# Moving columns of the up-projection in alternating runs, and padded w_in tiles, in a block-sparse attention + MLP kernel

## The chip, the cores and the metric

The kernel runs on one NeuronCore of a Trainium2 chip. The metric is device time in microseconds (us) for one execution. Engine names are those of the profile: PE is TensorE's matmul, PEld its weight load, DVE is VectorE, ACT is ScalarE, POOL is GpSimd, SP is SyncE, whose queue issues most of the DMAs.

## The reference

Block-sparse attention over 4 sequences of 768 tokens, 8 heads of 64, followed by a two-layer MLP on the 3072 tokens:

```python
scores = scale * np.matmul(q, k.transpose(0, 1, 3, 2))
...
attn_out = np.matmul(attn, v).astype(np.float32)
x = np.ascontiguousarray(attn_out.transpose(0, 2, 1, 3)).reshape(B * S, H * D)   # 3072 x 512
h = x @ w_in                                   # 512 -> 2048
g = h * (1.0 / (1.0 + np.exp(-1.702 * h)))
return (g @ w_out).astype(np.float32)          # 2048 -> 512
```

The mask keeps the first and last block row and column, the neighbours of the diagonal, and three sampled blocks per block row.

## The kernel before

The 3072 tokens are taken in NC = 6 chunks of CT = 512. The attention of a chunk is cut into items (scores, transposes, values, turn) that are laid between the steps of the MLP of the chunk before it, by a table (`plan`) in program order; the first chunk's attention comes ahead of the MLP in a handwritten order (`first`). TensorE executes its instructions in that written order.

The MLP runs over m = 0 to 95: m = 16 c + f, where c is the chunk and f one of NF = 16 slices of the 2048 hidden features. For each m, `up` makes h (128 features x 512 tokens) in one PSUM bank, `gate` applies the gelu (tanh on ACT, a product on DVE), `gate_hi` and `gate_lo` split the result in two, and one step later `down` multiplies it by w_out and sums over f in four other banks. The split into a high part (fp32r) and a low part is how single-pass matmuls reach the accuracy of fp32: a product is hi\*hi + hi\*lo + lo\*hi.

So one `up` is 4 values of k (128 rows of the 512 features each) times 3 matmuls (L565, L566, L567), 12 matmuls, each with a stationary 128 x 128 block of a w_in tile and 512 moving columns of x; the six chunks make 96 x 12 = 1152 of them. A w_in tile `win{f}` holds, in each partition, 1024 fp32 values: four 128-wide blocks of the high part, then four of the low part. The moving rows xhi and xlo (tile x1 in odd chunks) are 512 fp32 values, 2 KB, for each k. Both operands are read, and h is written, from front to back.

The tiles live in one SBUF pool that puts them one behind the other in the order in which they are made. A tile "pad" of 56 values near the front makes every large tile before the change start at a multiple of 2048 bytes; the w_in tiles stand there in the order win15 to win10, then win0 to win9, 4096 bytes each. The tiles win15 to win10 also lend their space, early on, to gathered value blocks (`spare` in `__init__`), before w_in arrives there.

Of the kernel before, what the change touches and what calls it, by code (L numbers as in the profile page):

```python
# [9 lines left out]
F32 = mybir.dt.float32  # L10
F32R = mybir.dt.float32r
I32 = mybir.dt.int32
# [6 lines left out]
P = 128  # L19
# [5 lines left out]
DM = H * D  # L25
DF = 2048
NCT = DM // P
NF = DF // P
# [13 lines left out]
AHEAD = 5  # L42
NFULL = 8
FIRST = CU // 2
ORDER = """X1 G0 G1 G2 G3 S0 S1 L0 E0 L1 X2 T0 E1 S2 S3 L2 C0 T1 C1 Y1 V0 N0 L3 X3 V1 E2 T2 R0 N1 E3 H0 S4 R1 S5 C2 T3 L4 H1
V2 N2 E4 C3 L5 Y2 T4 C4 R2 H2 E5 V3 N3 S6 L6 R3 G4 S7 H3 L7 E6 T5 V4 C5 Y3 V5 N4 E7 W W R4 T6 C6 N5 W R5 H4 H5 T7 C7 W
V6 N6 W V7 W R6 N7 H6 R7 H7 W W"""
# [2 lines left out]
class Kernel:  # L50
# [4 lines left out]
    def __init__(self, ctx, tc, q, qd, kb, kT, v, vd, sb, w_in, w_out, out):  # L55
        self.tc, self.nc = tc, tc.nc
        self.q, self.qd, self.kb, self.kT, self.v, self.vd, self.sb = q, qd, kb, kT, v, vd, sb
        self.w64, self.out = (w_in.bitcast(I32), w_out.bitcast(I32)), out
        pool = lambda name, bufs, **k: ctx.enter_context(tc.tile_pool(name=name, bufs=bufs, **k))
        self.const = pool("const", 1)  # L60
        self.work = pool("work", 2)
        self.small = pool("small", 6)
        psum = pool("psum", 1, space=PSUM)
        dram = pool("dram", 1, space=DRAM)
        self.ws = [dram.tile([P, DM], F32, name=f"ws{f}") for f in range(NF)]
        self.bank = [psum.tile([P, 512], F32, name=f"bank{i}") for i in range(8)]
        c = self.const


        self.sbr = c.tile([1, NB, NR, 2], I32, name="sbr")  # L70
        self.zero = c.tile([P, 1], F32, name="zero")
        self.seen = c.tile([P, 2 * NPAIR], F32, name="seen")
        self.ident = c.tile([P, P], F32, name="ident")
        self.vidx = c.tile([P, 2, NB], I32, name="vidx")
        self.bias = c.tile([P, NU, 8], F32, name="bias")
        c.tile([P, 56], F32, name="pad")

        self.kg = [c.tile([P, 12, 2, NPAIR * BLK], F32, name=f"kg{i}") for i in range(RING)]
        self.qt = [c.tile([P, 2, NPAIR * UT], F32, name=f"qt{i}") for i in range(RING)]
        self.vown = [c.tile([P, 2, 2 * DM], F32, name=f"vown{i}") for i in range(RING)]  # L80
        self.vmid = [c.tile([P, 2 * DM], F32, name=f"vmid{i}") for i in range(RING)]
        self.win = [None] * NF
        self.x = [tuple(c.tile([P, NCT, CT], F32R, name=f"x{part}0") for part in ("hi", "lo"))]


        more = c.tile([P, 2 * NCT * CT], F32, name="x1")
        nk, nq = 24 * NPAIR * BLK, 2 * NPAIR * UT
        for flat in (more[:, 0:nk], c.tile([P, 2 * WRING * DM], F32, name="wout")):
            self.kg.append(flat.rearrange("p (n b c) -> p n b c", n=12, b=2))
        self.qt += [more[:, nk + nq * i:nk + nq * (i + 1)].rearrange("p (b c) -> p b c", b=2) for i in range(2)]  # L90
        spare = [c.tile([P, 2 * DM], F32, name=f"win{NF - 1 - i}") for i in range(6)]
        self.vblocks = [[t[:, j] for j in range(2)] for t in self.vown] + [spare[0:2], spare[2:4]]
        self.vmid += spare[4:6]
        self.kmidof, self.vmidof = [None] * FIRST, [None] * FIRST
        self.units, self.kent, self.vent, self.items = [], [], [], []

        def entry(of, **more):
            of.append({"n": len(of), "scores": 0, "values": 0, **more})
            return of[-1]

        def item(k, v, **more):
            k["scores"] += 1
            v["values"] += 1
            self.items.append({"n": len(self.items), "unit": self.units[-1], "k": k, "v": v, **more})

        for b0 in range(0, B, 2):
            for u in range(NU):
                k, v = (entry(of, b=b0, u=u) for of in (self.kent, self.vent))
                for b in (b0, b0 + 1):
                    entry(self.units, b=b, u=u)  # L110
                    item(k, v, first=True, end=True)
            for b in (b0, b0 + 1):
                entry(self.units, b=b, u=None)
                k = entry(self.kent, b=b, u=None)
                for i in range(2):
                    v = entry(self.vent, b=b, u=None, i=i)
                    for half in range(2):
                        item(k, v, i=i, half=half, first=i + half == 0, end=i + half == 2)
        for of in (self.kent, self.vent):
            for e in of:  # L120
                e["at"] = e["n"] if e["n"] < FIRST else e["n"] % RING
        self.knext = self.vnext = FIRST
        self.most = {"scores": FIRST + 1, "values": FIRST + 1}
        self.early, self.turned = True, False
# [73 lines left out]
    def load_k(self, e):  # L198
# [18 lines left out]
        self.sampled(e, 0, nc.sync)  # L217
        if e["n"] >= FIRST or e["n"] == 0:
            self.sampled(e, 1, nc.sync if e["n"] else nc.scalar)
# [237 lines left out]
    def weights(self):  # L457

        nc = self.nc
# [7 lines left out]
        tiles = {}  # L467

        def fetch(k):
            if k < len(todo):  # L470
                f, i = todo[k]
                if i == 0:
                    raw = self.const.tile([P, 2 * DM], I32, name=f"win{f}")
                else:
                    raw = self.work.tile([P, 2 * DM], I32, name="raw", bufs=3)
                nc.gpsimd.dma_start(out=raw, in_=self.w64[i][f])
                tiles[k] = {"raw": raw.rearrange("p (a b) -> p a b", b=2)}
# [25 lines left out]
        for k, (f, i) in enumerate(todo):  # L503
            fetch(k + AHEAD)
            raw, a = tiles[k]["raw"], tiles[k]["a"]
            low, high = raw[:, :, 0], raw[:, :, 1]
            nc.vector.tensor_scalar(out=a, in0=a, scalar1=3, scalar2=None, op0=ALU.logical_shift_left)
            yield
            if k > 0 and "to" in tiles[k - 1]:
                rest(k - 1)  # L510
                yield
            nc.vector.scalar_tensor_tensor(out=a, in0=high, scalar=-0x80000000, in1=a, op0=ALU.bitwise_and,
                                           op1=ALU.bitwise_or)
            if k + 1 < len(todo):
                while todo[k + 1][1] == 1 and (not self.turned or todo[k + 1][0] - (4 if todo[k + 1][0] < NFULL else WRING) > self.downs - 1):
                    yield
                first(k + 1)
            yield
            w = a if (i, f >= NFULL) != (1, True) else raw.rearrange("p a b -> p (a b)")[:, 0:DM]
            nc.vector.scalar_tensor_tensor(out=w, in0=low, scalar=29, in1=a, op0=ALU.logical_shift_right,  # L520
                                           op1=ALU.bitwise_or)
            w = tiles[k]["w"] = w.bitcast(F32)
            if i == 0:
                self.win[f] = tiles[k]["to"] = self.const.tile([P, 2 * DM], F32R, name=f"win{f}")
            else:
                nc.sync.dma_start(out=self.ws[f], in_=w)
                if f < NFULL:
                    self.whole[f] = w
                    self.ready.add((f, i))
                else:  # L530
                    tiles[k]["to"] = self.wout[f % WRING]
            if "to" in tiles[k]:
                nc.scalar.copy(out=tiles[k]["to"][:, 0:DM], in_=w)
            yield
# [15 lines left out]
    def split(self, m):  # L550
        if m in self.wst:
            w, t = self.wst.pop(m), self.wout[m % WRING]
            self.nc.scalar.copy(out=t[:, 0:DM], in_=w)  # L553
            self.nc.vector.tensor_tensor(out=t[:, DM:2 * DM], in0=w, in1=t[:, 0:DM].bitcast(F32), op=ALU.subtract)  # L554

    def up(self, m, ks):
        nc = self.nc
        c, f = divmod(m, NF)
        if c == 0:
            self.need(f, 0)  # L560
        hi, lo = self.x[c % 2]
        wih, wil = (self.win[f][:, DM * k:DM * (k + 1)].rearrange("p (k m) -> p k m", k=NCT) for k in range(2))
        h = self.bank[2 if m == 1 else (7, 0)[m % 2] if c == NC - 1 else 7]
        for k in ks:
            nc.tensor.matmul(h, wih[:, k], hi[:, k], start=(k == 0), stop=False)  # L565
            nc.tensor.matmul(h, wih[:, k], lo[:, k], start=False, stop=False)  # L566
            nc.tensor.matmul(h, wil[:, k], hi[:, k], start=False, stop=(k == NCT - 1))  # L567
        self.h = h

    def gate(self, m, between):  # L570
# [323 lines left out]
```

## Time and profile before

| | |
|---|---|
| median of 2 runs | 761.75 us (761.07 to 762.42) |
| profiled execution | 762.78 us, of which the span from first to last instruction is 761.1 us |
| PE busy | 732.3 us, 96% of the span |
| DVE, ACT busy | 406.7 us (53%), 375.4 us (49%) |
| granted TensorE clock, mean | 0.992 |

In the profile a duration of a matmul runs from its start to the end of its drain, so that the durations of neighbours overlap. What a stream of matmuls costs is read from start to start, not from the durations. "Idle before" is time that the engine stood still ahead of an instruction, and the arrow names what ended it.

### The profile page before, as it was taken

The numbers are of one execution on the slowest core, as the hardware profiler recorded it, in microseconds if no ns is written. First come the engines' busy times: TensorE is split into PE (matmuls) and PEld (weight loads), VectorE is DVE, ScalarE is ACT, GpSimd is POOL, SyncE is SP. The second block draws the span as 40 slices with busy tenths as digits, with TensorE's granted clock in tenths as the row PEclk, the third lists the DMA queues.
The fourth block names the chain that finished last, engine by engine and source line by source line (L and its number), as shares of the span: only waits on it lengthen the run. The fifth ranks groups of instructions, "written<-read, shape, count | busy, mean of one in ns | idle before, by whom it ended". The sixth has DMA issues, their size and how long they took to land.

```text
span 761.1 us, 18922 instructions
## 1 busy us (share of the span) xinstructions
PE 732.3 (96%) x7424; PEld 564.8 (74%) x7424; DVE 406.7 (53%) x1069; ACT 375.4 (49%) x938; POOL 68.6 (9%) x111
## 2 busy tenths in 40 slices
PE   3779999999999999999999999999999999999997
PEld 2565666777787777778878878878777777888885
DVE  4578988895554434554454554454554444443333
ACT  3565667775554443544444545445545444333232
POOL 4332122020000000000000000000000000000000
PEclk9899999999999999999999999999999999999999
DMA  8998996775742547555435455435564331141111
GB/s 241 301 373 320 342 314 213 244 227 178 255 160 70 170 138 206 161 170 171 126 120 171 135 166 170 129 114 176 159 218 155 90 105 29 41 105 49 50 48 56
DMA packets 64251, 126.88 MB, mean 167 GB/s; under 512 B 7617, under 2 KB 30402, under 8 KB 63650
## 3 DMA queue, kind: packets, MB, share of 16 engines
q1 hardware_dynamic: 51922, 83.72, 36.3%
q0 software_dynamic: 11376, 41.03, 15.9%
q8 instruction: 58, 0.95, 0.5%
q10 hardware_dynamic: 864, 0.93, 0.4%
q14 instruction: 31, 0.25, 0.1%
HBM read 115.16 MB, written 10.49 MB: 165 GB/s over the span
## 4 chain that ended last, share of the span: by engine, by line
PE 92%; DMA 2%; SPq 2%; DVE 1%; issue 1%; ACT 1%; DVEq 0%
PE bank L565 13%; PE bank L566 11%; PE bank L567 11%; PE bank L624 10%; PE bank L625 10%; PE bank L620 10%; PE bank L354 6%; PE bank L378 6%; PE bank L303 5%; PE bank L610 4%; PE bank L398 2%; PE bank L315 2%; DMA x<-in_kb_dram 1%; PE bank L443 1%; SPq L225 1%
## 5 line engine op out<-in xcount | busy, mean ns | idle before, releaser
L580 DVE SCALAR_TENSOR_TENSOR g<-g,bank 128x512 f32<-128x512 f32 x83 | 57.0, 687 | 181.7 <-ACT g L573 181.7
L338 ACT ACTIVATE ex<-bank,nm 128x256 f32<-128x256 f32 (+1 forms) x176 | 84.6, 490 | 117.1 <-DVE nm L326 117.1
L624 PE MATMUL bank<-wout,ghi 128*128 128x512 f32 x352 | 139.8, 397 | 0.0
L625 PE MATMUL bank<-wout,ghi 128*128 128x512 f32 x352 | 137.2, 390 | 0.0
L573 ACT ACTIVATE g<-bank 128x512 f32<-128x512 f32 x96 | 57.3, 597 | 148.2 <-PE bank L567 148.2
L554 DVE TENSOR_TENSOR wout<-wst,wout 128x512 fp32r<-128x512 f32 x80 | 55.4, 692 | 79.9 <-ACT wout L553 78.8
L620 PE MATMUL bank<-wout,glo 128*128 128x512 f32 x352 | 97.1, 389 | 0.0
L326 DVE CUSTOM_DVE_ANT_1 bank<-bank,bias 128x256 f32<-128x256 f32 x176 | 73.7, 440 | 17.1 <-PE bank L303 10.5
L565 PE MATMUL bank<-xhi,win 128*128 128x512 f32 x192 | 80.3, 418 | 0.5 <-ACT xhi L450 0.5
L587 ACT CAST ghi<-g 128x512 fp32r<-128x512 f32 x88 | 54.7, 621 | 50.4 <-DVE g L580 50.4
L565 PE MATMUL bank<-x,win 128*128 128x512 f32 x192 | 78.3, 408 | 0.2 <-DVE g L580 0.2
L620 PEld LDWEIGHTS bank<-wout,glo 128*128 128x128 f32 x352 | 66.1, 188 | 13.9
L624 PEld LDWEIGHTS bank<-wout,ghi 128*128 128x128 f32 x352 | 66.1, 188 | 13.5
L625 PEld LDWEIGHTS bank<-wout,ghi 128*128 128x128 f32 x352 | 66.2, 188 | 13.0
L566 PE MATMUL bank<-xlo,win 128*128 128x512 f32 x192 | 75.4, 393 | 0.0
L567 PE MATMUL bank<-xhi,win 128*128 128x512 f32 x192 | 75.3, 392 | 0.0
L567 PE MATMUL bank<-x,win 128*128 128x512 f32 x192 | 75.1, 391 | 0.0
L566 PE MATMUL bank<-x,win 128*128 128x512 f32 x192 | 75.1, 391 | 0.0
L255 POOL DMA_INDIRECT vown<-in_v_dram,vidx x40 | 38.6, 965 | 378.3 <-PE bank L378 265.0
L359 ACT COPY pt<-bank 128x512 f32<-128x512 f32 (+1 forms) x112 | 56.8, 563 | 19.3 <-PE bank L354 19.3
L595 DVE TENSOR_TENSOR glo<-g,ghi 128x512 fp32r<-128x512 f32 x88 | 60.2, 684 | 1.4 <-ACT ghi L587 1.4
L303 PE MATMUL bank<-kg,qt 64*32 64x256 f32 x1280 | 46.0, 391 | 12.0 <-DMA vmid<-in_v_dram 12.0
(135 smaller groups left out, 1049.0 us busy)
## 6 DMA issues: line engine op xcount, KB each, us to landing
wst<-ws SPq DMA_DIRECT2D x80, 256.0 KB, 2.9
kg<-in_kb_dram SPq DMA_DIRECT2D x114, 128.0 KB, 2.9
kg<-in_kb_dram SPq DMA_DIRECT2D x42, 256.0 KB, 5.6
win<-in_moe_w_in_dram POOLq DMA_DIRECT2D x16, 512.0 KB, 7.1
raw<-in_moe_w_out_dram POOLq DMA_DIRECT2D x16, 512.0 KB, 5.3
kg<-in_kT_dram SPq DMA_DIRECT2D x4, 1536.0 KB
vown<-in_vd_dram SPq DMA_DIRECT2D x8, 768.0 KB, 4.9
out_dram<-raw SPq DMA_DIRECT2D x41, 128.0 KB, 2.3
```

Source lines behind the costliest of these rows:

```text
L303: nc.tensor.matmul(sps[h][BLK * c:BLK * (c + 1), n * i:n * (i + 1)].rearrange("p (g n s) -> p g n s", g=2, s=BLK), self.qt[r][rows, bi, UT ...
L326: nc.vector.tensor_tensor_reduce(out=at, in0=at, in1=bias, scale=-SCALE, scalar=3.0e38, op0=ALU.add, op1=ALU.min, accum_out=un["nm"][:, ha ...
L338: nc.scalar.activation(out=ex, in_=sps[h][:, n * k:n * (k + 1)], func=AF.Exp, bias=un["nm"][:, half, c:c + 1], scale=-1.0, accum_out=un["r ...
L565: nc.tensor.matmul(h, wih[:, k], hi[:, k], start=(k == 0), stop=False)
L566: nc.tensor.matmul(h, wih[:, k], lo[:, k], start=False, stop=False)
L567: nc.tensor.matmul(h, wil[:, k], hi[:, k], start=False, stop=(k == NCT - 1))
L573: nc.scalar.activation(out=g, in_=self.h, func=AF.Tanh, scale=0.851)
L580: nc.vector.scalar_tensor_tensor(out=g, in0=g, scalar=1.0, in1=h, op0=ALU.add, op1=ALU.mult)
L595: self.nc.vector.tensor_tensor(out=glo, in0=g, in1=ghi.bitcast(F32), op=ALU.subtract)
L620: nc.tensor.matmul(o[n], glo[:, tk[n]], woh, start=False, stop=last)
L624: nc.tensor.matmul(o[n], ghi[:, tk[n]], woh, start=(f == 0), stop=False)
L625: nc.tensor.matmul(o[n], ghi[:, tk[n]], wol, start=False, stop=False)
```

## The change

Two edits, which touch no other engine's program:

- each of the 16 w_in tiles is made 64 bytes longer per partition (PAD = 16 values), and only its first 4096 bytes are used. The tiles' starts, taken from the first of them, so move by 0, 64, 128, ... 960 bytes in the order win15 to win10, win0 to win9, and everything behind them moves by 1024 bytes;
- the three matmuls of `up` read the 512 moving columns, and write h, not from front to back but in runs that alternate between the two halves of the row (columns 0 to 255 and 256 to 511). A column's result lands at the same place as before. The tiles fall into four groups of four by their order in memory: runs of 16, second half first (win15 to win12); runs of 16, first half first (win11, win10, win0, win1); runs of 32, first half first (win2 to win5); runs of 32, second half first (win6 to win9).

```diff
+PAD = 16
...
-        spare = [c.tile([P, 2 * DM], F32, name=f"win{NF - 1 - i}") for i in range(6)]
+        spare = [c.tile([P, 2 * DM + PAD], F32, name=f"win{NF - 1 - i}")[:, 0:2 * DM] for i in range(6)]
...
-                    raw = self.const.tile([P, 2 * DM], I32, name=f"win{f}")
+                    raw = self.const.tile([P, 2 * DM + PAD], I32, name=f"win{f}")[:, 0:2 * DM]
...
-                self.win[f] = tiles[k]["to"] = self.const.tile([P, 2 * DM], F32R, name=f"win{f}")
+                self.win[f] = tiles[k]["to"] = self.const.tile([P, 2 * DM + PAD], F32R, name=f"win{f}")[:, 0:2 * DM]
...
+    def lines(self, ap, f):
+
+        n = (NF - 1 - f if f >= NF - 6 else 6 + f) // 4
+        ap = ap.rearrange("p (b a c) -> p a b c", b=2, c=(16, 16, 32, 32)[n])
+        return ap[:, ::-1] if n in (0, 3) else ap
+
...
+        to = self.lines(h, f)
         for k in ks:
-            nc.tensor.matmul(h, wih[:, k], hi[:, k], start=(k == 0), stop=False)
-            nc.tensor.matmul(h, wih[:, k], lo[:, k], start=False, stop=False)
-            nc.tensor.matmul(h, wil[:, k], hi[:, k], start=False, stop=(k == NCT - 1))
+            xh, xl = self.lines(hi[:, k], f), self.lines(lo[:, k], f)
+            nc.tensor.matmul(to, wih[:, k], xh, start=(k == 0), stop=False)
+            nc.tensor.matmul(to, wih[:, k], xl, start=False, stop=False)
+            nc.tensor.matmul(to, wil[:, k], xh, start=False, stop=(k == NCT - 1))
```

No instruction changes its place on any engine. What differs in the program is the shape of these matmuls. On PE, in the third chunk, the end of a sparse item's values and the beginning of the `up` of slice 6 (the name before the arrow is the PSUM bank, behind it the moving and the stationary tile) before the change:

```order
1622 L378 MATMUL bank_87<-vmid_106,pt 32x64 x4
1623 L378 MATMUL bank_87<-vown_104,pt 32x64 x4
1624 L565 MATMUL bank_92<-xhi_108,win_1551 128x512
1625 L566 MATMUL bank_92<-xlo_109,win_1551 128x512
1626 L567 MATMUL bank_92<-xhi_108,win_1551 128x512
```

and after it:

```order
1622 L379 MATMUL bank_87<-vmid_106,pt 32x64 x4
1623 L379 MATMUL bank_87<-vown_104,pt 32x64 x4
1624 L574 MATMUL bank_92<-xhi_108,win_1551 128x8x2x32
1625 L575 MATMUL bank_92<-xlo_109,win_1551 128x8x2x32
1626 L576 MATMUL bank_92<-xhi_108,win_1551 128x8x2x32
```

The rows stand at the same numbers; an output of 512 columns has become 8 times 2 runs of 32 (in the tiles of the first two groups, 16 times 2 runs of 16).

## Rows read from the trace of the kernel before

**Rows 1.** The page: busy time by engine, and granted clock in 40 slices.
```profile
PE 732.3 (96%) x7424; PEld 564.8 (74%) x7424; DVE 406.7 (53%) x1069; ACT 375.4 (49%) x938; POOL 68.6 (9%) x111
...
PEclk9899999999999999999999999999999999999999
```

**Rows 2.** Busy time by stage: stretch, its length, then each engine, granted clock, DMA.
```profile
0.00:57.00 57.00, 36.11 (x720) 26.05 (x720) 32.17 (x137) 30.49 (x96) 22.89 (x53) 0.91 0.96 305
57.00:182.00 125.00, 122.65 (x1321) 85.99 (x1322) 106.50 (x254) 80.77 (x196) 23.21 (x34) 1.00 0.80 271
...
330.00:500.00 170.00, 170.00 (x1842) 135.53 (x1841) 81.57 (x218) 81.24 (x203) 10.30 (x11) 1.00 0.48 145
...
660.00:761.00 101.00, 96.13 (x425) 79.18 (x423) 37.45 (x57) 32.10 (x56) 0.00 (x0) 0.99 0.22 60
```

**Rows 3.** The chain that ended last, its shares of the span by engine.
```profile
PE 92%; DMA 2%; SPq 2%; DVE 1%; issue 1%; ACT 1%; DVEq 0%
```

**Rows 4.** Groups of the page: the two steps that wait for `up`.
```profile
L580 DVE SCALAR_TENSOR_TENSOR g<-g,bank 128x512 f32<-128x512 f32 x83 | 57.0, 687 | 181.7 <-ACT g L573 181.7
...
L573 ACT ACTIVATE g<-bank 128x512 f32<-128x512 f32 x96 | 57.3, 597 | 148.2 <-PE bank L567 148.2
```

**Rows 5.** Timeline of PE, last chunk: start us, duration us, instruction.
```profile
699.72 0.39 PE L566 MATMUL bank<-x,win 128*128 128x512 f32 x1
699.95 0.39 PE L567 MATMUL bank<-x,win 128*128 128x512 f32 x1
...
701.31 0.39 PE L567 MATMUL bank<-x,win 128*128 128x512 f32 x1
```

**Rows 6.** The same stretch for PEld, the weight loads.
```profile
699.73 0.19 PEld L567 LDWEIGHTS bank<-x,win 128*128 128x128 f32 x1
699.95 0.19 PEld L565 LDWEIGHTS bank<-x,win 128*128 128x128 f32 x1
```

**Rows 7.** Timeline of PE, an `up` of the second chunk behind attention matmuls.
```profile
280.92 0.50 PE L565 MATMUL bank<-x,win 128*128 128x512 f32 x1
281.26 0.40 PE L566 MATMUL bank<-x,win 128*128 128x512 f32 x1
281.50 0.40 PE L567 MATMUL bank<-x,win 128*128 128x512 f32 x1
...
283.58 0.39 PE L567 MATMUL bank<-x,win 128*128 128x512 f32 x1
```

**Rows 8.** The chain in order of time: start us, us on the chain, what.
```profile
67.84 1.02 PE bank L303 x32
...
71.81 3.43 PE bank L610 x8
```

**Rows 9.** Groups of the page: busy us, mean ns of one, idle before.
```profile
L566 PE MATMUL bank<-xlo,win 128*128 128x512 f32 x192 | 75.4, 393 | 0.0
L567 PE MATMUL bank<-xhi,win 128*128 128x512 f32 x192 | 75.3, 392 | 0.0
L567 PE MATMUL bank<-x,win 128*128 128x512 f32 x192 | 75.1, 391 | 0.0
L566 PE MATMUL bank<-x,win 128*128 128x512 f32 x192 | 75.1, 391 | 0.0
```

**Rows 10.** One line in detail (L567): duration ns, min/median/max.
```profile
L567 PE MATMUL bank<-x,win x192: 387/389/398, 183.3 to 750.3; 128*128 128x512 f32 x192
```

**Rows 11.** DMA issues: count, KB each, median us to landing.
```profile
win<-in_moe_w_in_dram POOLq DMA_DIRECT2D x16, 512.0 KB, 7.1
```

**Rows 12.** The chain again, later: a dense item's scores.
```profile
254.99 0.81 PE bank L315 x8
```

**Rows 13.** Weight loads by size: busy us, mean ns of one, idle before.
```profile
L565 PEld LDWEIGHTS bank<-x,win 128*128 128x128 f32 x192 | 36.0, 188 | 8.7 <-DVE g L580 0.4
L378 PEld LDWEIGHTS bank<-vown,pt 128*32 128x32 f32 x1216 | 27.9, 110 | 0.5 <-issue 0.3
...
L398 PEld LDWEIGHTS bank<-vown,pt 128*64 128x64 f32 x384 | 12.5, 137 | 9.1 <-issue 6.7 <-DVE glo L595 2.4
```

## Prediction

> **What bounds the kernel now.** I read the busy times first: PE is busy for 96% of the span, DVE and ACT for about half of it [rows 1]. An average can hide stages, so the busy time by stage comes next: up to 57 us the kernel waits for loads and the first attention, with PE busy for 36 of 57 us; from there on PE is busy for 122.65 of 125.00 us, then without a gap, then for 96 of the last 101 [rows 2]. The chain of what ended last says the same: 92% of it is PE [rows 3]. The reader is to see that behind 57 us the time is the sum of PE's start-to-start distances, and that all 1152 matmuls of `up` lie there. The steps that wait for `up`, tanh and the product, idle 148 and 182 us in all [rows 4], so they don't push back. A nanosecond gained or lost on each matmul of `up` moves the end by 1152 ns.
>
> So the question is what one such matmul costs, and what share of that the order of its columns can touch. In the last chunk, where nothing interrupts the stream, the start of L566 at 699.72 and that of L567 at 701.31 are seven matmuls apart: 1.59 / 7 = 227 ns [rows 5]. 512 columns at the granted clock (1.00 in the middle stages [rows 2], the 2.4 GHz level) would be 213.3 ns. So 14 ns of each matmul are neither columns nor a wait for a semaphore. A weight load starts with each matmul and takes 190 ns of the 227 [rows 6], so it isn't late; but it reads SBUF while the moving columns are read. Two rows say that the 14 ns can change. Behind attention matmuls the same instructions stand at distances of up to 240 ns (281.26 to 281.50), and ten of them (281.26 to 283.58) at 232 ns on average, with no wait listed [rows 7]. And the fp32 form of L610 takes 3.43 / 8 = 429 ns for each of its eight instructions [rows 8]: 2 ns more than two column times (426.7), although each has a weight load too. The excess belongs to the form that takes a 4-byte column in every cycle, and it varies with something other than the amount of work.
>
> The mean over all of `up`: a listed duration of 389 ns goes with a distance of 227 (the last chunk's pattern, and the median [rows 5, 10]), and the four large groups of L566 and L567 average (393 + 392 + 391 + 391) / 4 = 391.75 [rows 9], 2.75 more. I take 227 + 2.75 = 230 ns for every matmul of `up`.
>
> **The change, part by part.**
> *Padding.* It adds no instruction and no byte of transfer: 16 loads of 512 KB, 7.1 us each [rows 11], land in rows 64 bytes further on. They are issued long before their tile is used, beside the other early loads. Price taken: 0. If a load took 10% longer, 0.7 us would be hidden by the conversion work ahead of the first `up`; only the first loads could show at all, so at most about 1 us.
> *Same columns, other order.* Neither the number of matmuls nor of columns changes, no wait is added, and the result lands where tanh reads it as before. What is left is the distance of 230 ns, and no row of before shows an alternating order of this form. Bounds from the nearest rows:
> - Below: all interference between weight load and columns goes away, and the excess falls to the 2 ns of L610 [rows 8]. 213.3 + 2.1 = 215.4 against 230: 14.6 ns, times 1152 = 16.8 us less. The first chunk's 192 matmuls may not pass their gain on, since DVE is busy for 106 of 125 us there [rows 2]; for the other 960 it is 14.0 us.
> - Above, from rows: every matmul at the worst distance of the interrupted stream, 240 ns [rows 7]: 10 x 1152 = 11.5 us more.
> - Reading in runs by itself: the scores of sparse items (L303) read their columns in runs of 32 that jump, those of dense items (L315) without a jump. 32 instructions of 256 columns, eight at a time, take 1.02 us, so 255 ns a round, 1.00 ns a column [rows 8]; 8 of 384 columns, four at a time, take 0.81 us, 405 ns a round, 1.05 ns a column [rows 12]. The jumps of the reader cost nothing that shows. I take 0.
> - Writing in runs: every PSUM output of PE before is in one piece, so no row has its price. It is the one part that could go beyond the bound above (rival 2).
>
> I take 0 for the sum. The reason is the evenness of the stream: in the last chunk the weight and column tiles, k, high and low parts all change from matmul to matmul, and the distance stays 227 [rows 5]. An excess made by one address meeting another would be expected to differ between them. It speaks against this that all large tiles start at multiples of 2048 bytes, so that their relative position was never really varied; hence a forecast of no change is a choice, and the gain stays a strong rival.
>
> The Trainium skill bears on this, in "SBUF — State Buffer", section "Who interferes with whom": PE has two independent read ports, one for the moving operand and one for the weight load, and never waits on anyone. By that rule the gain below would be 0, and the sum stays as it is. The distances of 227 to 240 without a listed wait [rows 7] show that something inside does vary; they don't show that it is the reads.
>
> **The rivals.**
> *1. The alternating order removes the interference (faster).* A weight load of 32 columns takes 110 ns, of 64 137, of 128 188 [rows 13]: some 0.8 ns a column, where a moving column takes 0.42. Front to back, the columns are so read at twice the rate of the weight block beside them, and the two readers pass each other again and again. In alternating runs the position within a half moves at half speed, about as fast as the weight block is read: whatever distance they have, they keep. If the excess is a meeting of the two, a matmul that has once been shifted clear stays clear. Full price: 14.0 to 16.8 us less, 746.0 to 748.8; if half the tiles profit, 8 us less, 755. For it: the 14 ns that the fp32 form doesn't have [rows 5, 8]. Against it: the evenness above, and 16 different starts, some of which would be bad ones.
> *2. A jump in the output costs PE time (slower).* The place is the write into the bank of h: half the tiles jump 32 times in a row of 512, half 16 times, 24 on average. One column time (0.42 ns) a jump is 24 x 0.42 = 10 ns, 11.5 us in all, 774.3; two are 23 us, 785.8. 2% of the time (15.2 us, or 13.2 ns a matmul) is reached from 13.2 / 24 = 0.55 ns a jump. For it: no row shows such a write as free. Against it: the reader's jumps of the same length are free, and within a run the columns are neighbours.
> The skill has a rule that speaks for this rival: "PSUM — Partial Sum Buffer", section "Specifications (TRN2)", says that PSUM lines are 8 bytes and that any access that isn't contiguous slows matmuls significantly. It gives no figure; taken at its word the kernel would be slower by more than rival 2's first step. No row here tests it.
> *3. The order of the stream is lost (a little slower).* The steady 227 may be a favourable footing that the equal alignment of all tiles gives; with 16 starts, many may have the 232 to 240 that follow an interruption. (232 - 230) x 1152 = 2.3 us to 11.5 us more, 765 to 774.
>
> **How the numbers follow.** The sum is made against the profiled execution, 762.8 us, of which 761.1 is the span; it lies 1 us over the median, so no change means about 762 in a new median. Chances: no change, within 4 us: 0.42. Rival 1: 0.25, of which 0.05 pass 2%. Rival 3: 0.19. Rival 2: 0.14, nearly all of it past 2%. The predicted time is the likeliest case's, 762.0. The range takes in most of the gain (down to 748) and the bound of 11.5 us with a little of rival 2 (up to 778), and leaves out about 0.07 below and 0.12 above. About 2% is what a measurement of this kernel can tell from no change: faster by more 0.05, within 0.81, slower by more 0.14.
>
> **What would show it.** In the profile after, the distances from start to start of the matmuls of `up` in the last chunk decide, tile by tile, against 227: 216 in some or all tiles is rival 1; over 235 with the tiles in runs of 16 worse than those in runs of 32 is rival 2, since the price goes by the jump; a spread of 227 to 240 that goes by the tile's start, not by the run length, is rival 3. The matmuls of `down`, whose order is unchanged, should stay at 227; PE's busy time should move by the same amount as the end; and the stretch before 57 us should stay. I am wrong as a whole if the end moves with `up` unchanged, which would mean that padding touched the loads or the tiles behind w_in, which now start 1024 bytes further on.

## The result, and the profile after

The changed kernel takes 770.68 us in the median of 2 runs (768.26 to 773.11), against 761.75 us: a ratio of 1.0129, 95% interval 1.0098 to 1.0160. It is slower by some 9 us, clear of the noise and inside the 2% that the forecast counted as no change. The profiled execution took 773.11 us with a span of 771.5.

One thing about the change has to be put right first. In the first and the last group of tiles the index that is reversed is that of the runs, not that of the halves. So these tiles are read from the row's end backwards: the last run of the first half, the last run of the second half, the run before it of the first half, and so on. "Second half first", in the part on the change above, is wrong; below these orders are called backwards.

The page after: busy time by engine, the chain by engine, and the groups that answer to [rows 9], and one of `down`.

```profile
PE 743.6 (96%) x7424; PEld 565.1 (73%) x7424; DVE 407.0 (53%) x1069; ACT 375.3 (49%) x938; POOL 68.6 (9%) x111
...
PE 92%; DMA 2%; SPq 2%; issue 1%; ACT 1%; DVE 1%; DVEq 0%; ACTq 0%
...
L633 PE MATMUL bank<-wout,ghi 128*128 128x512 f32 x352 | 140.5, 399 | 0.0
...
L575 PE MATMUL bank<-xlo,win 128*128 128x512 f32 x192 | 76.5, 399 | 0.0
L576 PE MATMUL bank<-x,win 128*128 128x512 f32 x192 | 76.5, 398 | 0.0
L576 PE MATMUL bank<-xhi,win 128*128 128x512 f32 x192 | 76.5, 398 | 0.0
L575 PE MATMUL bank<-x,win 128*128 128x512 f32 x192 | 76.5, 398 | 0.0
```

PE is busy 11.3 us longer, no other engine by more than 0.4 us, and the chain has no new wait: the same matmuls take longer. The mean durations of `up` rise from 391 to 393 ns [rows 9] to 398 to 399. To see where, the time is cut at the first `up` matmul of each chunk (the last stretch ends at the last `up` matmul). Before, PE alone (stretch, length, busy time and instructions, granted clock, DMA share, GB/s):

```profile
57.38:182.87 125.49, 123.52 (x1325) 1.00 0.80 270
182.87:312.56 129.69, 129.14 (x1329) 1.00 0.53 161
312.56:427.02 114.46, 114.46 (x1240) 1.00 0.49 148
427.02:541.59 114.57, 114.57 (x1238) 1.00 0.52 156
541.59:666.18 124.59, 124.59 (x1194) 1.00 0.36 112
666.18:750.27 84.09, 84.09 (x372) 1.00 0.21 57
```

and after:

```profile
58.51:185.41 126.90, 124.70 (x1324) 1.00 0.79 264
185.41:316.20 130.79, 130.24 (x1330) 1.00 0.51 160
316.20:432.24 116.04, 116.04 (x1239) 1.00 0.48 146
432.24:548.40 116.16, 116.16 (x1239) 1.00 0.50 154
548.40:674.10 125.70, 125.70 (x1193) 1.00 0.33 111
674.10:760.50 86.40, 86.40 (x372) 1.00 0.19 55
```

Each chunk is 1.1 to 2.3 us longer, 9.1 us in sum, at the same granted clock; the last one, where nothing else is mixed in, most. The stretch ahead of the first `up` is 1.1 us longer here, but 56.5 us in the run with padding alone and 56.7 in the one with the orders alone, so that part is scatter between executions.

Inside the last chunk the distances go by the tile's order. Timeline of PE after, start and duration of two matmuls of each tile; first tile win2 (runs of 32), then win11 (runs of 16 forwards), then win12 (runs of 16 backwards):

```profile
685.58 0.40 PE L575 MATMUL bank<-x,win 128*128 128x512 f32 x1
...
687.95 0.40 PE L576 MATMUL bank<-x,win 128*128 128x512 f32 x1
...
735.89 0.41 PE L575 MATMUL bank<-x,win 128*128 128x512 f32 x1
...
738.30 0.40 PE L576 MATMUL bank<-x,win 128*128 128x512 f32 x1
...
741.53 0.39 PE L575 MATMUL bank<-x,win 128*128 128x512 f32 x1
...
743.82 0.39 PE L576 MATMUL bank<-x,win 128*128 128x512 f32 x1
```

Each pair of rows is ten matmuls apart: 237, 241 and 229 ns, against 227 in the same chunk before [rows 5].

The table gives the mean distance from start to start for every tile in the last chunk (the last eight matmuls of the `up`, each to the start of the next), worked out from the start times in the traces of this kernel and of the first four experiments. "fwd" stands for runs read forwards, "back" for backwards. The four numbers of a group are the tiles whose start lies 0, 64, 128 and 192 bytes behind a multiple of 256 (all 0 where nothing is padded).

```
ns                 win15..12: 16 back     win11,10,0,1: 16 fwd   win2..5: 32 fwd        win6..9: 32 back
before (no runs)   227 227 227 227        227 227 227 227        227 227 227 227        227 227 227 227
whole change       233 236 229 229        240 240 240 240        237 237 237 236        237 237 236 237
padding alone      227 233 233 229        227 233 233 229        227 233 232 229        227 233 233 229
orders alone       233 233 233 233        240 240 240 240        237 237 237 237        237 237 237 237
order, read only   233 236 229 229        240 240 240 240        237 237 237 236        237 237 236 237
order, write only  227 233 233 229        227 233 233 229        227 233 232 229        227 233 233 229
```

These are distances of an unbroken stream. In the second to fifth chunk an `up` stands behind matmuls of the attention. There the tiles of the kernel before stand anywhere from 227 to 232 ns themselves, and padding adds only 0.2 to 0.3 us to a chunk, against 1.0 us to the last.

The matmuls of `down`, whose program is unchanged, grow behind such an `up` and then come back. Timeline of PE after, the `down` behind win11:

```profile
738.54 0.40 PE L633 MATMUL bank<-wout,ghi 128*128 128x512 f32 x1
...
740.39 1.07 PE L629 MATMUL bank<-wout,glo 128*128 128x512 f32 x4
741.30 0.39 PE L574 MATMUL bank<-x,win 128*128 128x512 f32 x1
```

The first eight matmuls take 1.85 / 8 = 231 ns each, the last four 0.91 / 4 = 228; in the last chunk before, all of them stand at 227.

### The profile page after: what moved, and what is told of

Its sections match the earlier page's. It is cut to its first block, busy times and chain, and to the rows that moved or that the text cites. A ratio compares the mean times of both kernels' runs of the same rounds, so it can differ in the third digit from the quotient of the medians.

```text
span 771.5 us, 18908 instructions
## 1 busy us (share of the span) xinstructions
PE 743.6 (96%) x7424; PEld 565.1 (73%) x7424; DVE 407.0 (53%) x1069; ACT 375.3 (49%) x938; POOL 68.6 (9%) x111
## 4 chain that ended last, share of the span: by engine, by line
PE 92%; DMA 2%; SPq 2%; issue 1%; ACT 1%; DVE 1%; DVEq 0%; ACTq 0%
PE bank L574 13%; PE bank L575 12%; PE bank L576 12%; PE bank L633 10%; PE bank L634 10%; PE bank L629 10%; PE bank L355 6%; PE bank L379 6%; PE bank L304 5%; PE bank L619 4%; PE bank L399 2%; PE bank L316 2%; PE bank L444 1%; DMA x<-in_kb_dram 1%; SPq L226 1%
## 5 line engine op out<-in xcount | busy, mean ns | idle before, releaser
L582 ACT ACTIVATE g<-bank 128x512 f32<-128x512 f32 x96 | 57.4, 598 | 155.7 <-PE bank L576 155.7
L574 PE MATMUL bank<-xhi,win 128*128 128x512 f32 x192 | 81.4, 424 | 0.5 <-ACT xhi L451 0.5
L574 PE MATMUL bank<-x,win 128*128 128x512 f32 x192 | 79.6, 414 | 0.2 <-DVE g L589 0.2
L576 PE MATMUL bank<-x,win 128*128 128x512 f32 x192 | 76.5, 398 | 0.0
L576 PE MATMUL bank<-xhi,win 128*128 128x512 f32 x192 | 76.5, 398 | 0.0
L575 PE MATMUL bank<-x,win 128*128 128x512 f32 x192 | 76.5, 398 | 0.0
L360 ACT COPY pt<-bank 128x512 f32<-128x512 f32 (+1 forms) x112 | 56.7, 563 | 20.4 <-PE bank L355 20.4
```

What stands on the lines that cost most here:

```text
L574: nc.tensor.matmul(to, wih[:, k], xh, start=(k == 0), stop=False)
L575: nc.tensor.matmul(to, wih[:, k], xl, start=False, stop=False)
L576: nc.tensor.matmul(to, wil[:, k], xh, start=False, stop=(k == NCT - 1))
L582: nc.scalar.activation(out=g, in_=self.h, func=AF.Tanh, scale=0.851)
```

## The experiments

**Padding alone** (e1_pad_only). The tiles stay padded; `lines` returns its argument.

```diff
     def lines(self, ap, f):
-        n = (NF - 1 - f if f >= NF - 6 else 6 + f) // 4
-        ap = ap.rearrange("p (b a c) -> p a b c", b=2, c=(16, 16, 32, 32)[n])
-        return ap[:, ::-1] if n in (0, 3) else ap
+        return ap
```

Expected: 

> Padded tiles, columns front to back. Start theory (the shifted starts of the w_in tiles spoil the stream's footing): last-chunk distances of the up matmuls spread over 227 to 240 ns from tile to tile, 766 to 771 us. Order theory (only the alternating order costs, in the read or in the write): 227 ns in every tile, 762 us. Meeting theory (a weight read and a column read that meet): small differences between tiles, each tile within 224 to 236 ns, 760 to 766 us.

Measured: 763.88 us, ratio 1.0033 (1.0012 to 1.0053). The distances repeat with every fourth tile, that is with the start in 256 bytes: 227, 233, 233, 229. Two matmuls of win14 (64 bytes on), ten apart (233 ns), in the timeline of PE:

```profile
743.84 0.39 PE L573 MATMUL bank<-x,win 128*128 128x512 f32 x1
...
746.17 0.39 PE L574 MATMUL bank<-x,win 128*128 128x512 f32 x1
```

The order theory, with 227 everywhere, falls; so does the start theory's size. Starts at multiples of 256 bytes are the good ones here, and padding has a small price of its own, inside what the meeting theory allowed.

**Orders alone** (e2_order_only): `PAD = 0`.

Expected: 

> The four orders, no padding (all w_in tiles at multiples of 2048 bytes as before). Start theory: back to 227 ns and 762 us. Order theory: the same distances as with the whole change, 240 ns for runs of 16 forwards, 236 to 237 for runs of 32, 228 to 231 for runs of 16 backwards, 770 us. Meeting theory: the groups change places, above all at least one of them by more than 5 ns, since a constant distance between the two readers now is 0 in every tile; 765 to 778 us.

Measured: 769.50 us, ratio 1.0115 (1.0085 to 1.0146). Nearly all of the price is in the orders. With padding and without, forward runs of 16 stand at 240 and runs of 32 at 236 to 237; of the four orders the start matters only for runs of 16 backwards (233 here at start 0, 229 to 236 with padding). No group moved by more than 5 ns against the whole change, which the meeting theory had wanted.

**Read and write apart** (e3_read_only, e4_write_only). In the first the output of the matmul is h from front to back, cut to the same shape; in the second the columns are read from front to back.

```diff
-        to = self.lines(h, f)
+        c = self.lines(h, f).shape[-1]
+        to = h.rearrange("p (a b c) -> p a b c", b=2, c=c)
```

```diff
-            xh, xl = self.lines(hi[:, k], f), self.lines(lo[:, k], f)
+            xh, xl = (t[:, k].rearrange("p (a b c) -> p a b c", b=2, c=to.shape[-1]) for t in (hi, lo))
```

Expected of the read: 

> Padded tiles; the columns are read in the alternating orders, but h is written front to back (so the tokens of h stand permuted, by tile; the output is another one). Write theory (a jump in the PSUM output costs PE time): 227 ns in every tile, 762 us. Read theory (the alternating read costs, by itself or with the weight load): distances as with the whole change, 229, 240, 237, 237 ns by group, 770 us.

Expected of the write: 

> Padded tiles; the columns are read front to back, but h is written in the alternating orders (tokens of h permuted, by tile; the output is another one). Write theory: distances as with the whole change, 770 us. Read theory: 227 ns in every tile, or as with padding alone, 762 us.

Measured: the read alone 769.43 us, ratio 1.0123 (1.0095 to 1.0151); the write alone 762.41 us, 1.0028 (1.0012 to 1.0045), which is the price of padding. Tile win11 in the timeline of the read alone, ten matmuls apart (240 ns):

```profile
730.30 0.41 PE L576 MATMUL bank<-x,win 128*128 128x512 f32 x1
...
732.70 0.40 PE L577 MATMUL bank<-x,win 128*128 128x512 f32 x1
```

and in that of the write alone (226 ns):

```profile
726.64 0.39 PE L575 MATMUL bank<-x,win 128*128 128x512 f32 x1
...
728.90 0.39 PE L576 MATMUL bank<-x,win 128*128 128x512 f32 x1
```

What goes beyond padding is all in the read. Writes to PSUM in runs of 16 or 32 that jump between the halves of a bank cost nothing that shows (762.41 us, against 763.88 with the same padding and writes from front to back). The rule of the Trainium skill ("PSUM — Partial Sum Buffer", section "Specifications (TRN2)") that any access that isn't contiguous slows matmuls significantly does not hold for runs of this length, and the measurement decides.

**A scan of orders** (e5_scan_orders). No padding, each tile with an order of its own, read only, as above.

Expected: 

> No padding; each of the 16 w_in tiles is read in an order of its own, h is written front to back (tokens permuted by tile; the output is another one). Meeting theory (the distance depends on how fast the place that the column read is at, within 256 bytes, passes the place that the weight read is at): the whole row backwards differs from forwards by 3 ns or more; in alternating halves forwards and backwards differ for runs of 8 and 4 as for 16 (240 against 233 ns); orders in blocks backwards go with the whole row backwards. Jump theory (each jump of the read costs a fixed time): forwards and backwards alike, and the price goes with the number of jumps: runs of 8 about 13 ns over those of 16, runs of 64 and 128 within 3 ns of 227, the row backwards 227. Some order below 222 ns would show that the excess can be removed by order alone.

The kernel took 784.85 us in one run, beside 759.93 before; some 16 of the 25 us are the tile with every second column. Where a kernel has one run, that carries no verdict on the time: the kernel before itself went from 758.48 to 763.99 us in 19 runs. What is read is the distances.

Distances in the last chunk, worked out from the start times as in the table above. "Halves in turn" are the alternating runs of the change, "blocks of 16 backwards" is the whole row in pieces of 16, last piece first, each read forwards:

```
front to back; halves swapped; blocks of 64 backwards                    226.6
halves in turn: runs of 128 fwd; of 64 fwd; of 64 back                   226.6
quarters in turn, runs of 16 fwd                                         232
whole row backwards; blocks of 16 backwards; blocks of 4 backwards       233.2
halves in turn: runs of 16 back                                          233.4
halves in turn: runs of 8 fwd, 8 back                                    243, 252
halves in turn: runs of 4 fwd, 4 back                                    250, 253
every second column, then the others                                     453
```

Timeline of PE: runs of 64 backwards (eleven matmuls apart, 226 ns), then every second column (eleven apart, 452 ns):

```profile
728.22 0.39 PE L586 MATMUL bank<-x,win 128*128 128x512 f32 x1
...
730.71 0.39 PE L588 MATMUL bank<-x,win 128*128 128x512 f32 x1
...
761.16 0.61 PE L586 MATMUL bank<-x,win 128*128 128x512 f32 x1
...
766.13 0.63 PE L588 MATMUL bank<-x,win 128*128 128x512 f32 x1
```

Pieces of at least 64 columns, 256 bytes, were free in all five orders tried with them; in pieces of 4 to 32 columns the order costs. Jumps alone don't explain it: the row backwards has no jump and takes 7 ns more, and runs of 8 differ by 9 ns between forwards and backwards. The meeting theory had these two right, but it put the blocks of 64 backwards with the row backwards, and they are free; at runs of 4 the two directions are only 3 ns apart; and backwards is the better direction at runs of 16, the worse one at runs of 8 and 4. No order goes below 226.6. Every second column takes twice the time although the number of columns is the same, so a read of this form is not paid by the column alone. What it is paid by, and why just these orders cost, no run here shows.

**Finer starts** (e6_fine_starts). `PAD = 8` (32 bytes), front to back in the first eight tiles in memory, runs of 16 backwards in the other eight.

Expected: 

> Padding of 32 bytes instead of 64: eight tiles read front to back at starts of 0 to 224 bytes in 256, eight in runs of 16 backwards at the same eight starts. Meeting theory: front to back the distances at 0, 64, 128, 192 are those with 64 bytes of padding (226.6, 233, 232.5, 229 ns) and the ones between lie within 224 to 236; runs of 16 backwards, where both readers keep their distance, vary more with the start than front to back, by 8 ns or more, one start at 229 or below. Jump theory: runs of 16 backwards all alike.

Distances in the last chunk by start, in ns:

```
start in 256 bytes     0    32    64    96   128   160   192   224
front to back        227   233   233   234   233   233   229   232
runs of 16 back      233   234   236   229   229   228   229   234
```

The values of 64 bytes of padding come back. Runs of 16 backwards vary by 7.8 ns, just short of the 8 asked for, with a low stretch from 96 to 192. The kernel took 762.51 us in one run, beside 759.93 before.

**The columns moved instead of the weights** (e8_shift_x). A tile of 192 bytes ahead of xhi and xlo of the even chunks, and one of 64 bytes behind them, which brings all else back to multiples of 256.

```diff
+        c.tile([P, 48], F32, name="shift")
         self.x = [tuple(c.tile([P, NCT, CT], F32R, name=f"x{part}0") for part in ("hi", "lo"))]
+        c.tile([P, 16], F32, name="rest")
```

Expected: 

> The kernel before with xhi and xlo of the even chunks moved by 192 bytes; x1 (odd chunks), wout and all w_in tiles stay at multiples of 256 bytes. Relative theory (the place of the columns against that of the weights, within 256 bytes, decides): even chunks as the tiles that padding puts 64 bytes on, about 233 ns, odd chunks 226.6 in the last chunk. Weight-start theory (only where the weight block starts counts): even chunks 228 to 229.5 as before.

Measured: 764.24 us in one run, beside 761.69. Timeline of PE, chunk 4, tile win1, six matmuls apart, 233 ns:

```profile
551.47 0.39 PE L568 MATMUL bank<-xlo,win 128*128 128x512 f32 x1
...
552.87 0.39 PE L568 MATMUL bank<-xlo,win 128*128 128x512 f32 x1
```

The even chunks stand at 233 to 234 ns on average (in a steady 233, or 231 and 236 in turn), the last chunk at 226.6. So the place of the columns counts, and not that of the weights alone. Moving the columns on by 192 bytes gave what moving the weights on by 64 gives, which is the same place of one against the other within 256 bytes. That fits the relative theory but doesn't prove it: only one shift was tried, and weight starts from 32 to 160 bytes all give about 233. The rule of the Trainium skill that PE's two read ports make it wait on nothing ("SBUF — State Buffer", section "Who interferes with whom"), by which neither shift would matter, differs from this measurement (233 ns against 226.6).

**Smaller and other weight loads** (e7_small_loads, e9_load_lines). In the first, nine of the twelve matmuls load 96 or 64 stationary columns; in the second all load 128, but one and the same value of a row (`broadcast_to`) or every second value of a stretch twice as long.

```diff
-            nc.tensor.matmul(h, wih[:, k], hi[:, k], start=(k == 0), stop=False)
...
+            n = P if k == 0 else 96 if f < 8 else 64
+            for w, x, stop in ((wih, hi, False), (wih, lo, False), (wil, hi, k == NCT - 1)):
+                nc.tensor.matmul(h[0:n], w[:, k, 0:n], x[:, k], ...
```

Expected of the smaller loads: 

> The kernel before, but of the twelve matmuls of an up only the first three load 128 stationary columns; the other nine load 96 (tiles 0 to 7) or 64 (tiles 8 to 15), so part of the sum is left out and the output is another one. All of them stream 512 columns as before. Load theory (the 13 ns over 512 column times are taken by the weight load that reads beside the columns): in the last chunk about 223 ns with 96 columns and 220 with 64. Form theory (the 13 ns belong to the matmul's form, whatever is loaded): 227 ns everywhere.

Measured: 762.41 us in one run beside 761.69. The last chunk doesn't stand at 223 and 220 but varies from 228 to 233 with 96 columns (mean 230) and from 224 to 236 with 64 (mean 229). Both theories fall: less to load takes nothing off, and the even stream of 227 is lost.

Expected of the other blocks: 

> The kernel before with other stationary blocks of 128 columns, so that the output is another one: in tiles 0 to 7 all 128 columns are one and the same value of a row (one 16-byte place read again and again), in tiles 8 to 15 every second value of a stretch of 1024 bytes (twice as many places as before). Weight-read theory (what the weight load reads meets what the columns read): the two halves differ from the 227 ns of the kernel before in the last chunk and from each other by 4 ns or more. Form theory (the excess over 213 ns belongs to the columns' own reading): 227 ns in all tiles.

Measured: 765.08 us in one run, beside a median of 760.41. One value: 234, 233, 226 in turn, mean 231; every second value: 233. What the weight load reads does change the distance, by 4 and 7 ns, with the number of columns loaded unchanged. The two halves differ by only 2 ns, where 4 were expected, so the weight-read theory is met in one of its two points.

**Alternating halves without a price** (e10_runs_of_64): `PAD = 0`, and `c=64` in place of `(16, 16, 32, 32)[n]`.

Expected: 

> No padding, all tiles in alternating halves with runs of 64 columns, half of them forwards and half backwards, h written in the same order. If the price of the change is the order of the read within 256 bytes, this order is free: 227 ns in the last chunk, 760 to 763 us. If alternating between the halves costs by itself: over 230 ns, 765 us or more.

Measured: 760.78 us against 760.41, ratio 1.0007 (0.9990 to 1.0024), 227 ns in every tile of the last chunk. It is no better than the kernel before; no run was.

## Why the prediction was right in its range and wrong in its likeliest case

The time lies in the range and in the class that had 0.81, but the case that gave the number, no change within 4 us, did not come: it is 9 us more.

- *What bounds the kernel* was right: PE alone grew, chunk by chunk, and nothing off it pays. The mean distance of matmuls of `up` that follow each other rose from 229.5 (230 in the prediction) to 235.8 ns; 6.3 x 1152 = 7.3 us. Those of `down` were to stay and rose from 227.5 to 229.4, 1.9 x 1056 = 2.0 us. Together 9.3, where the six stretches have 9.1. The first matmuls of `down` behind a disturbed `up` take part in the disturbance, as the rows behind win11 show. The scan of orders has the control: behind the tiles that stand at 226.6 the `down` of the last chunk is at 227 from its start, behind the others its first eight are at 228 to 232.
- *Padding at nothing* was right on what it priced: the loads don't show, and the stretch ahead of the first `up` didn't grow (56.5 us with padding alone, 57.4 before). It left out the starts, which cost 0.3%; the prediction has them in rival 3 only.
- *"The jumps of the reader cost nothing that shows. I take 0"* is the step that failed. The rows behind it, L303 against L315 [rows 8, 12], are of the slower fp32 form: 1.00 and 1.05 ns a column there, where `up` takes 227 / 512 = 0.44. For the form of `up` runs of 32 cost 10 ns, and the orders alone 1.15%. That the slower form has time to spare for such a read may be the reason; no run tried these orders with that form.
- *The evenness of 227 ns* was read as a sign against a meeting of addresses. It was none: within 256 bytes every large tile had the same place, and as soon as that was varied, by padding or by moving x, the distances varied. The prediction named this weakness and then went with the evenness.
- *Rival 1* (faster) rested on a read that keeps its distance to the weights. No order and no start went below 226.6, and the order built to keep it, runs of 16 forwards, is the worst of the whole change, at 240 at every start. Backwards the distance varies with the start (228 to 236 in the last chunk) and is lower; so if one order keeps its distance, it is that one, but no run shows that any does.
- *Rival 2* (the write) is refuted by the write alone. The mark that it was given, runs of 16 worse than runs of 32, was met by the forward tiles (240 against 237) without its cause: the same mark fits a price of the read.
- *Rival 3* came nearest. Its range of 765 to 774 holds the result, and the even 227 was a favourable footing. But it put the loss on the starts, which carry 0.3%, and not on the order of the read; that the number fits is luck.

What stays open: what the 13 ns between 213 and 226.6 are, and why a given place costs just what it does. Weight loads of half the size don't lower them, and other stationary blocks change them. The start within 256 bytes isn't all of it either, since the same tile can stand on different levels: win14, read backwards, is at 228 in the third to fifth chunk of the changed kernel and at 236 in the last.

## What to carry to other kernels

Where single-pass 4-byte matmuls of 512 columns are the bound, keep moving and stationary tiles at the same place within 256 bytes and read the columns in pieces of at least 256 bytes from front to back; here that kept the distance at 227 ns, while runs of 4 to 32 columns cost 2 to 26 ns more. The order in which the output is written cost nothing at the runs of 16, 32 and 64 columns tried here. And a price read from another form of the same instruction need not carry over: that form took over twice the time for a column, and the price that didn't show there was 10 ns here.

## What was not expected of the hardware

- The distance of such matmuls, in an unbroken stream, depends on where the weight block starts within 256 bytes: 227, 233, 233, 229 ns at 0, 64, 128, 192 bytes. It depends on where the columns start too: 233 with x moved by 192.
- Taking every second 4-byte column, then the others, doubles the time, 453 against 227 ns.
- A whole row read backwards costs 7 ns more than forwards; in blocks of 256 bytes backwards it costs nothing.
- PSUM writes in jumping runs of 16 columns are free: 227, 233, 233, 229 ns at the four starts, as with writes from front to back.
